# Two LayerNorms behind the residual adds, one row's residual moved to VectorE, one row's moments to ScalarE, in the token stage of a spectral and attention stack

## The chip, the cores and the metric

One core of one Trainium2 chip. The metric is the device time of the whole program in microseconds (us). The time before is 1554.5 us, the median of 3 runs from 1554.37 to 1554.54. The state of an execution (fast or slow) was judged by its time and granted clock.

## The reference

A stack of two kinds of layer, each with a LayerNorm and a residual, run twice: layer A is a two-dimensional Fourier transform, a product with complex weights and the inverse transform; layer B is attention over 64 segments that hand a memory of 8 rows on to each other.

```python
def _layernorm(x, axis=-1, eps=1e-05):
    m = jnp.mean(x, axis=axis, keepdims=True)
    v = jnp.var(x, axis=axis, keepdims=True)
    return (x - m) / jnp.sqrt(v + eps)

def _A_ref(x, w_r, w_i):                       # x: 1 x 2048 x 640
    X = jnp.fft.rfft2(x.astype(jnp.float32), axes=(-2, -1)) * (w_r + 1j * w_i)
    return jnp.fft.irfft2(X, s=(S, D), axes=(-2, -1)).astype(jnp.bfloat16)

# ... _B_ref: 64 segments of 32 rows, 32 heads of 128, memory of 8 rows ...
x = A_x
x = x + _A_ref(_layernorm(x), A_w_r, A_w_i)
x = x + _B_ref(_layernorm(x), B_mem0, ...)
x = x + _A_ref(_layernorm(x), A_w_r, A_w_i)
x = x + _B_ref(_layernorm(x), B_mem0, ...)
```

## The kernel before

The change touches the token stage, which is the end of layer A and the beginning of layer B. The 2048 tokens are 16 "rows" of 128 tokens by 640 columns. For each row TensorE does the last transform (`psg`, then `psy`, tiles in PSUM, the memory in which TensorE leaves its sums), the residual is added, mean and variance are taken, and the row is normalised and transposed for the projections of layer B. A "norm" here always means the two normalising passes of a pair of rows (norm 2 is rows 4 and 5), "inverse 2" the inverse root that norm 2 needs, and an evacuation is the copy of a finished transpose out of its PSUM buffer. The residual of a row can be added by TensorE (two matmuls with the identity, then a copy by ScalarE) or by VectorE, for the rows in `ADDED`. The moments of a row can be taken by VectorE (`bn_stats`, `bn_aggr`) or, for the rows in `SQUARED`, by a sum that the add gives as a by-product, scaled by GpSimd, and a Square on ScalarE.

```python
LEAD, LAG, EARLY, LAST = 0, 7, 10, 10
ADDED, SQUARED = (0, 1, 2, 3, 4, 6), (1, 3, 6) + (15,)

def tokens(s0):
    ...
    psy = pp.tile([128, 2, 512], FP32, name="psy", tag="pg", bufs=3)
    by_dve = s0 in ADDED
    for a in range(0 if by_dve else 2):
        nc.tensor.matmul(psy[:, a, 0:320], lhsT=g["ident"][:], rhs=x[:, s0, a * 320:(a + 1) * 320], start=True, stop=False)
    ...                                        # four transform matmuls into psy
    acc = nm[:, s0:s0 + 1] if s0 in SQUARED else None
    if by_dve and acc is None:
        nc.vector.tensor_tensor(out=xr, in0=psy[:, :, 0:320], in1=xr, op=ALU.add)
        flush()                                # bn_aggr of the row whose statistics are pending
    elif by_dve:
        nc.vector.scalar_tensor_tensor(out=xr, in0=psy[:, :, 0:320], scalar=1.0, in1=xr, op0=ALU.mult, op1=ALU.add, accum_out=acc)
        flush()
    elif acc is None:
        nc.scalar.copy(out=xr, in_=psy[:, :, 0:320])
    ...

def act_stats(s0):
    m, n = mv[s0 // 2][:, s0 % 2, :], nm[:, s0:s0 + 1]
    if s0 < 15:
        nc.gpsimd.tensor_scalar_mul(out=n, in0=n, scalar1=-D ** -1.5)
    ...
    nc.scalar.activation(out=xna[:, s0, :], in_=x[:, s0, :], func=ACTF.Square, scale=D ** -0.5, bias=n, accum_out=m[:, 1:2])
    nc.gpsimd.tensor_scalar_mul(out=m[:, 0:1], in0=n, scalar1=-D ** 0.5)

# _inverse, as GpSimd runs it for a pair of rows: six instructions on 128x2 elements
small.tensor_scalar_add(out=t, in0=v, scalar1=LN_EPS)
small.tensor_tensor(out=r0, in0=t, in1=g["half"][:, 0:t.shape[1]], op=ALU.pow)
...                                            # two products, one a*t+b, one product

with tc.manual_schedule(engines={nc.tensor.engine, nc.scalar.engine, nc.vector.engine}):
    moved, late, by_dve_jobs = [], [], False
    turn = lambda s0: s0 + (2 if LEAD <= s0 < LAG else 1)
    for i in range(16 + 1):
        held = moved if by_dve_jobs else []    # evacuations of the transposes of the step before
        for f in moved if not held else moved[:1]:
            f()
        held, moved = held[1:], []
        ...
        if not early and i % 2 == 1:
            norm((i - 5) // 2)                 # steps 11, 13, 15: norms 3, 4, 5
        if not last:
            ready(False)                       # statistics on VectorE
        if i < 16:
            spectrum_d(i)                      # psg of row i, and its copy by ScalarE
        ready(True)                            # moments on ScalarE
        for f in held:
            f()
            flush()
        for s0 in range(16):
            if turn(s0) == i:
                tokens(s0)
        if early and i >= 5 and i % 2 == 1:
            norm((i - 5) // 2)                 # steps 5, 7, 9: norms 0, 1, 2
        ...
        if i >= 4 and i % 2 == 0:
            inverse((i - 4) // 2, nc.gpsimd)
        ...
        if i >= 8 and i % 4 < 3:               # transposes of a group of four rows
            n = i % 4
            ...
```

The order of TensorE, ScalarE and VectorE is the order in which this is written; GpSimd's instructions are placed by a scheduler.

## Time and profile before

| | before |
|---|---|
| median of 3 runs | 1554.5 us |
| span of the profiled execution | 1552.9 us |
| granted TensorE clock | 0.999 |
| TensorE busy, whole span | 99% |
| the two token stages | 73 to 110 us and 835 to 872 us |

In a profile line of an engine's order of time, the first number is the start, the second the duration, then engine, source line, operation, output and inputs, shapes, count. A bracket at the end is idle time of the engine just before, with the instruction that ended it. In the chain of waits each line is one piece of the chain that ended last. PE is TensorE, DVE VectorE, ACT ScalarE, POOL GpSimd. L134 is the normalising pass, L633 the add with a sum, L630 the add without, L650 the statistics, L658 their aggregate, L663 GpSimd's scaling of a sum, L124 to L129 the inverse root on GpSimd, L607 the `psg` matmuls. Helpers that stand below the change have numbers one higher in the kernel after: L1676, L1680 and L1661 before are L1677, L1681 and L1662 after.

I use one yardstick from within a trace, the **stage length**: from the start of the first `psg` matmul to the start of the last normalising pass. Before, it is 33.16 us in the first token stage and 33.14 in the second.

### The profile page before, as it was taken

Reading aid. Unit: us, or ns where it says so; the run is one execution under the profiler, and the core shown is the slowest. Engines: PE = TensorE matmul, PEld = TensorE weight load, DVE = VectorE, ACT = ScalarE, POOL = GpSimd, SP = SyncE. Lnnn points to the kernel's source line nnn. Section 1 sums busy time; section 2 is a strip of 40 time slices with the busy share of each in tenths; the row PEclk is TensorE's granted clock in tenths of the full one; section 3 lists DMA queues with packets and bytes.
Section 4 is the critical chain, followed back from the end, with each engine's and each line's share of the span. In section 5 each row is a group of like instructions: output and inputs, shape, how many; then the busy total and the mean of one; then the engine's idle time right before and its main releaser. Section 6 shows DMA issues by size and latency. Waiting matters only on the chain.

```text
span 1552.9 us, 36725 instructions
## 1 busy us (share of the span) xinstructions
PE 1535.5 (99%) x14554; PEld 1081.3 (70%) x14555; DVE 816.6 (53%) x2418; ACT 764.9 (49%) x2229; POOL 246.0 (16%) x337
## 2 busy tenths in 40 slices
PE   9999999999999999999999999999999999999997
PEld 7776666666666666777777776666666666667775
DVE  7873555555556545632368545654556545553111
ACT  5574655556555565511126655556555565562000
POOL 2530111112111121100035201112111121110000
PEclk9999999999999999999999999999999999999999
DMA  4780343344533444645114523443434434337241
GB/s 173 230 299 27 111 170 122 137 140 135 178 123 136 136 136 149 201 117 162 51 54 159 178 83 125 136 150 121 172 124 140 148 125 166 124 107 228 79 127 53
DMA packets 168839, 214.90 MB, mean 138 GB/s; under 512 B 8144, under 2 KB 134360, under 8 KB 168656
## 3 DMA queue, kind: packets, MB, share of 16 engines
q1 hardware_dynamic: 168080, 210.15, 40.9%
q8 instruction: 116, 1.90, 0.5%
q0 software_dynamic: 576, 2.30, 0.4%
q14 instruction: 67, 0.55, 0.1%
HBM read 167.32 MB, written 45.10 MB: 137 GB/s over the span
## 4 chain that ended last, share of the span: by engine, by line
PE 92%; DVE 4%; POOL 1%; ACT 1%; issue 1%; DMA 0%; ACTq 0%; DVEq 0%; POOLq 0%
PE psv L1267 19%; PE psk L1201 19%; PE psx L1547 18%; PE psq L1201 18%; PE pso L1351 4%; PE pss L1277 4%; PE ab L449 2%; PE psl L1304 1%; PE psq L1225 1%; PE X L480 1%; PE psu L541 1%; DVE lnst L650 1%; PE psm L977 1%; PE psg L1708 1%; PE psvb L1640 1%
## 5 line engine op out<-in xcount | busy, mean ns | idle before, releaser
L1201 PEld LDWEIGHTS <-bB_S 128*128 128x128 bf16 x3180 | 261.5, 97 | 181.3 <-issue 1.1
L1260 DVE CAST bB_S<-psk 128x495 bf16<-128x495 f32 (+3 forms) x320 | 191.6, 599 | 281.3 <-PE psk L1201 276.9
L1547 PE MATMUL psx<-Wo_sb,bB_S 128*128 128x320 bf16 x2048 | 288.7, 299 | 0.1
L1280 ACT ACTIVATE bB_S<-pss 128x269 bf16<-128x269 f32 (+5 forms) x576 | 208.7, 387 | 138.3 <-PE pss L1277 137.9
L1547 PEld LDWEIGHTS <-bB_S 128*128 128x128 bf16 x2048 | 196.8, 98 | 73.9 <-DVE bB_S L1365 0.7
L1320 POOL TENSOR_TENSOR bB_S<-bB_S,bB_S 128x535 f32<-128x535 f32 x90 | 111.7, 1254 | 795.2 <-DVE bB_S L1312 762.2
L1245 ACT ACTIVATE bB_S<-psq 128x96 bf16<-128x96 f32 x300 | 152.1, 507 | 172.6 <-PE psq L1201 172.6
L1365 DVE TENSOR_TENSOR bB_S<-pso,bB_S 128x480 bf16<-128x480 f32 (+1 forms) x320 | 193.0, 603 | 55.8 <-PE pso L1351 47.2
L1281 DVE TENSOR_TENSOR bB_S<-bB_S,maskf 128x269 bf16<-128x269 bf16 (+5 forms) x576 | 159.5, 290 | 114.3 <-ACT bB_S L1280 114.3
L1269 ACT CAST bB_S<-psv 128x512 bf16<-128x512 f32 (+1 forms) x288 | 162.4, 564 | 81.0 <-PE psv L1267 81.0
L1267 PE MATMUL psv<-bB_S,B1hT_S 128*128 128x256 bf16 x1360 | 168.8, 272 | 0.0
L1267 PE MATMUL psv<-bB_S,B2hT_S 128*128 128x256 bf16 x1360 | 168.8, 272 | 0.0
L1201 PE MATMUL psk<-B1hT_S,bB_S 128*128 128x495 bf16 (+3 forms) x800 | 164.2, 343 | 0.0
L1201 PE MATMUL psk<-B2hT_S,bB_S 128*128 128x495 bf16 (+3 forms) x800 | 164.2, 343 | 0.0
L1201 PE MATMUL psq<-B1hT_S,bB_S 128*128 128x495 bf16 (+5 forms) x780 | 156.0, 336 | 0.5 <-DVE bB_S L1646 0.5
L1201 PE MATMUL psq<-B2hT_S,bB_S 128*128 128x495 bf16 (+5 forms) x780 | 156.0, 336 | 0.5 <-DVE bB_S L1646 0.5
L1267 PEld LDWEIGHTS <-B1hT_S 128*128 128x128 bf16 x1360 | 129.8, 98 | 24.3
L1267 PEld LDWEIGHTS <-B2hT_S 128*128 128x128 bf16 x1360 | 129.8, 98 | 24.3
L1277 PE MATMUL pss<-bB_S 128*128 128x132 bf16 (+8 forms) x1152 | 137.5, 219 | 0.0
L1277 PEld LDWEIGHTS <-bB_S 128*128 128x128 bf16 x1152 | 95.4, 97 | 55.1
L1351 PE MATMUL pso<-bB_S,bB_S 128*128 128x132 bf16 (+8 forms) x1152 | 118.6, 219 | 0.2
L1351 PEld LDWEIGHTS <-bB_S 128*128 128x128 bf16 x1152 | 89.7, 98 | 32.3 <-DVE oTmf L1366 1.9
(299 smaller groups left out, 1438.5 us busy)
## 6 DMA issues: line engine op xcount, KB each, us to landing
bB_S<-Rd SPq DMA_DIRECT2D x124, 535.0 KB
oTx_d<-bB_S SPq DMA_DIRECT2D x60, 512.0 KB
bB_S<-oTx_d SPq DMA_DIRECT2D x46, 512.0 KB
bB_S<-in_B_Wq_dram SPq DMA_DIRECT2D x32, 320.0 KB
bB_S<-in_B_Wk_dram SPq DMA_DIRECT2D x32, 320.0 KB
bB_S<-in_B_Wv_dram SPq DMA_DIRECT2D x32, 320.0 KB
Wo_sb<-in_B_Wo_dram SPq DMA_DIRECT2D x4, 1280.0 KB
B1wv_S<-in_B_Wv_dram SPq DMA_DIRECT2D x10, 512.0 KB
```

Source lines behind the costliest of these rows:

```text
L1201: nc.tensor.matmul(ps, lhsT=w[:, ch, hh * 128:(hh + 1) * 128], rhs=src[:, ch, lo:hi], start=(ch == 0), stop=(ch == 4))
L1245: nc.scalar.mul(out=qv[:, :, 0:SEG], in_=x_view(ps, o, n)[:, :, 1:SW], mul=scale)
L1260: nc.vector.tensor_copy(out=KTs[h % 2][:, lo:hi], in_=ps[:, 0:hi - lo])
L1267: nc.tensor.matmul(ps[:, i * 256:(i + 1) * 256], lhsT=hT[:, ch, st.hcol((t + i) * 128):st.hcol((t + i) * 128) + 128], rhs=w["Wv"][:, ch, : ...
L1269: nc.scalar.copy(out=V[:, t:t + n, :].rearrange("p a b -> p (a b)"), in_=ps[:, 0:n * 256])
L1277: nc.tensor.matmul(ps[:, off - o0:off - o0 + hi - lo], lhsT=KT[:, t * 128:(t + 1) * 128], rhs=QT[:, lo:hi], start=True, stop=True)
L1280: nc.scalar.activation(out=E[:, 0:n], in_=ps[:, 0:n], func=ACTF.Exp)
L1281: nc.vector.tensor_tensor(out=P[:, o0:o0 + n], in0=E[:, 0:n], in1=bs.mask[:, o0:o0 + n], op=ALU.mult)
L1320: nc.gpsimd.tensor_tensor(out=acc, in0=acc, in1=part, op=ALU.add)
L1351: nc.tensor.matmul(pso[:, lo - q0:hi - q0], lhsT=V[:, t, (h % 2) * 128:(h % 2 + 1) * 128], rhs=P[:, off:off + hi - lo], start=(i == 0), st ...
L1365: nc.vector.tensor_tensor(out=oT.rearrange("p (r s j) -> p r s j", r=16, j=2)[:, :, s0:s0 + ns, :], in0=byclass(po), in1=rx, op=ALU.mult)
L1547: self.tc.nc.tensor.matmul(ps[:, 0:320], lhsT=lhs(h, k // 2), rhs=self.g["Wo_sb"][:, h, c0:c0 + 320], start=(h == 0), stop=(h == H - 1))
```

## The change

The intent: TensorE, VectorE and GpSimd wait for each other in the middle of the stage, because a norm that waits for GpSimd stands in VectorE's queue ahead of the residual add that TensorE needs. So norms 0 and 1 go behind the adds of rows 4 and 6 (steps 6 and 8 rather than 5 and 7), the transposes of the first four rows one step later (9, 10, 11), row 5's residual goes from TensorE to VectorE, and row 4's moments from VectorE to ScalarE.

```diff
--- before.py
+++ after.py
@@ -608,7 +608,7 @@
             nc.scalar.copy(out=Gs[s0 % 3], in_=psg[:, :, 0:NF])
 
         LEAD, LAG, EARLY, LAST = 0, 7, 10, 10
-        ADDED, SQUARED = (0, 1, 2, 3, 4, 6), (1, 3, 6) + (15,)
+        ADDED, SQUARED = tuple(range(7)), (1, 3, 4, 6) + (15,)
         nm = wk.tile([128, 16], FP32, name="lnnm", tag="lnnm")
 
         def tokens(s0):
@@ -688,13 +688,14 @@
                 if late:
                     late.pop(0)()
                 last = i >= LAST
+                due = {6: 0, 8: 1}.get(i, (i - 5) // 2 if i >= 9 and i % 2 else None)
                 early = i < EARLY
                 done = [s0 for s0 in range(16) if turn(s0) == i - 1]
                 ready = lambda act: [stats(s0) for s0 in done if (s0 in SQUARED) == act and s0 < 15]
                 if last:
                     ready(False)
-                if not early and i % 2 == 1:
-                    norm((i - 5) // 2)
+                if not early and due is not None:
+                    norm(due)
                 if not last:
                     ready(False)
                 if i < 16:
@@ -706,8 +707,8 @@
                 for s0 in range(16):
                     if turn(s0) == i:
                         tokens(s0)
-                if early and i >= 5 and i % 2 == 1:
-                    norm((i - 5) // 2)
+                if early and due is not None:
+                    norm(due)
                 for f in late:
                     f()
                 late = []
@@ -722,8 +723,8 @@
                 if i == 16:
                     for s0 in range(10):
                         handoff.add_u(pp, xna[:, s0, :], s0)
-                if i >= 8 and i % 4 < 3:
-                    n = i % 4
+                if 9 <= i < 12 or i >= 12 and i % 4 < 3:
+                    n = i % 4 - (i < 12)
                     by_dve_jobs = n != 1 and i < 16
                     jobs = handoff.rows_out(handoff.rows_in(pp, xna, i // 4 - 2, 2 * n), by_dve_jobs)
                     if n == 1:
```

## The prediction

> **What bounds the kernel now.** I read the page first, then the chain of waits, then the order of time of each engine between 72 and 114 us.
>
> ```profile
> span 1552.9 us, 36725 instructions
> PE 1535.5 (99%) x14554; PEld 1081.3 (70%) x14555; DVE 816.6 (53%) x2418; ACT 764.9 (49%) x2229; POOL 246.0 (16%) x337
> PE 92%; DVE 4%; POOL 1%; ACT 1%; issue 1%; DMA 0%; ACTq 0%; DVEq 0%; POOLq 0%
> ```
>
> TensorE carries 92% of the chain, nearly all in attention, which the diff does not touch. The change is in the token stage, which runs twice. It begins with the first transform matmuls (psg) at 73.06 and 835.02 us and ends with the last row transposes near 110 and 872. What the two stages hold comes from the busy time by stretches:
>
> ```profile
> 73.00:110.00 37.00, 35.70 (x400) 26.03 (x398) 29.48 (x84) 29.01 (x56) 15.07 (x58) 1.00 0.87 299
> 835.00:872.00 37.00, 35.72 (x402) 26.05 (x400) 29.48 (x84) 29.02 (x56) 15.06 (x58) 1.00 0.86 300
> ```
>
> (Columns: length, then busy us with count of PE, PEld, DVE, ACT, POOL, then clock, DMA share, GB/s.) The stages are copies of each other: 74 us, 4.8% of the span. A 2% change of the whole, 31 us, would need 42% of them. So only "same" is in play, and the question is tenths of a microsecond.
>
> Within a stage the chain of waits passes TensorE, GpSimd (the norm's inverse root), then VectorE almost without a gap:
>
> ```profile
> 86.04 0.20 POOL lnrs L129
> 86.24 0.03 issue
> 86.27 0.45 DVE A1tok_S L134
> ...
> 91.29 0.20 POOL lnrs L129
> 91.49 0.03 issue
> 91.52 0.80 DVE A1tok_S L134 x2
> ...
> 101.38 0.76 DVE lnst L650 x2
> 102.13 0.34 DVE A1tok_S L134
> 102.48 0.13 DVE lnmv L658
> ```
>
> The reader should see that VectorE is the chain from 91.52 to 102.61 us. TensorE is near it, not ahead. Two idle times on VectorE lie before that, seen in its order of time:
>
> ```profile
> 82.58 0.80 DVE L134 TENSOR_SCALAR A1tok_S<-A1x_S,lnmv,lnrs 128x640 bf16<-128x640 bf16 x2 [0.69 <-POOL lnrs L129]
> 83.29 0.17 DVE L1626 COPY B1hT_S<-psm 128x40 bf16<-128x40 bf16 x1
> 83.38 0.17 DVE L1627 COPY gqf<-psm 128x5 bf16<-128x5 bf16 x1
> 83.45 0.82 DVE L630 TENSOR_TENSOR A1x_S<-psy,A1x_S 128x640 bf16<-128x640 f32 x1
> ...
> 86.27 0.45 DVE L134 TENSOR_SCALAR A1tok_S<-A1x_S,lnmv,lnrs 128x640 bf16<-128x640 bf16 x1 [1.08 <-POOL lnrs L129]
> ```
>
> Row 4's residual add stands behind the first norm, which waits for GpSimd until 82.54. The add frees a PSUM buffer that TensorE wants:
>
> ```profile
> 84.32 0.99 PE L607 MATMUL psg<-A1gt_S,A1UT_S 128*128 128x321 bf16 x6 [0.35 <-DVE A1x_S L630]
> ```
>
> That gap, 83.82 to 84.32 between issues, is the clearest one to win.
>
> **What the Trainium skill says.** (1) "TensorE: Matmul & The Clock Gate", its opening table of specifications: the queues of ScalarE, VectorE and GpSimd are strict first-in-first-out. The trace agrees: the add at 83.45 was runnable at about 82.3 and ran after the waiting norm. (2) "VectorE: DVE Perf Modes", section Why PSUM operands drop a tier: fp32 from PSUM runs at the basic rate. The trace agrees: the add takes 0.82 us for 640 columns, against 0.36 between issues for the norm's bf16 pass. (3) Same page, section Two Vector instructions with no wait between them: an accumulator output is a second instruction. The trace has it, 84 ns. (4) "SBUF — State Buffer", section SBUF: two separate sides: VectorE and GpSimd share one port pair as an exclusive lock. The trace agrees as far as it goes: GpSimd's tiny scaling of the sums took 0.43 us beside the norm pass at 82.6, and 0.23 elsewhere.
>
> **The change, part by part, for each stage.** I built the changed kernel and listed each engine's instruction order.
> - Row 5's residual moves from TensorE to VectorE. This takes away two identity matmuls at 0.137 us spacing (0.27) and one ScalarE copy (about 0.6 between issues), and gives VectorE an add of 0.82.
> - Row 4's moments move from VectorE to ScalarE: VectorE loses two statistics passes and an aggregate (0.80 + 0.12), gains an accumulator read (0.08); ScalarE gains a Square with read (0.82 between issues); GpSimd gains two small instructions (0.23 + 0.07 each).
> - Sums: TensorE -0.27, VectorE -0.02, ScalarE +0.2, GpSimd +0.6. So work hardly falls; what counts is the order.
> - Order: norm 0 now comes behind row 4's add (step 6), norm 1 behind row 6's add (step 8), both before the odd-step norm 2 at step 9. The first group's three transposes come one step later, in steps 9, 10, 11.
>
> Now I walk the new order by hand with the old durations. Up to 81.8 us nothing changes.
> - VectorE: row 4's last matmul issues at 82.03 and takes 0.30, so the add runs 82.36 to 83.2 rather than from 83.45. Then norm 0 (0.71) to 83.9, row 5's add to 84.75, row 5's statistics to 85.55, row 6's add to 86.4, aggregate to 86.5.
> - TensorE: row 5 without its residual ends issue at 83.54. The buffer was freed at 83.2, so the next psg starts at 83.54 in place of 84.32: 0.78 gained, of which 0.27 is removed work and 0.5 removed wait.
> - GpSimd: inverse 1 still needs row 3's Square (84.02), now with one row-4 instruction inside it: end 86.54, not 86.24. Norm 1 runs 86.57 to 87.3, hard behind row 6's add: the old 1.08 us wait is filled.
> - GpSimd then runs inverse 2 at once. It needs row 5's aggregate (86.5) and follows row 6's scaling: start about 86.93, plus the old length of this sequence with one instruction inside it (89.06 to 91.49, 2.43), end 89.37. So norm 2 starts about 89.40 instead of 91.52: 2.12 earlier. VectorE idles here, after row 7's statistics (88.07), for 1.3 us.
> - From norm 2 on, VectorE is full. Between norm 2's start and the first copy of the transposes of rows 4 to 7 the old kernel takes 91.52 to 96.63, 5.11. The new one has to do, additionally, the evacuation of the first transposes (two copies of 0.64, one of 0.25) and row 7's aggregate (0.12), and saves about 0.1 three times, where an aggregate or small copy no longer follows directly on what it reads: 5.11 + 1.65 - 0.3 = 6.46. It reaches the same point at 95.86, against 96.63: **0.8 us gained**.
> - From there both orders are the same to the end of the stage.
>
> TensorE must keep up. It reaches step 11's third transpose about 91.86, but that needs the buffer of the first, emptied by VectorE only at 92.6: a new stall near 0.8 us. After it TensorE finishes the transposes of rows 4 to 7 at about 94.97, against 95.84: 0.87 gained, just enough not to starve VectorE. ScalarE's last chain (row 15: copy, Square, logarithm, exponential) follows TensorE, 0.85 earlier. GpSimd's inverse 6 follows VectorE, 0.8 earlier. All three meet at the last two norms, so the whole tail moves by 0.8.
>
> Two stages, 2 x 0.8 = 1.6 us. Layer B begins when these end; the chain there shows no DMA, so the gain should pass through: 1554.5 - 1.6 = **1552.9 us**.
>
> **The rivals.**
> - The new wait eats it: TensorE stalls at step 11 for the transpose buffer. For: VectorE empties it behind norm 2. Against: VectorE is the later one anyway. If it is longer than I think by 0.5 us, VectorE starves and the gain falls to 0.3 a stage: 1553.9.
> - GpSimd becomes the bound: inverse 1 and 2 run back to back with four more small instructions in the two stages, and port collisions with norm passes doubled such instructions (0.43). For: norm 2 waits for it. Against: 2.1 us of lead. Three collisions of 0.2 would leave 0.2 a stage: 1554.1.
> - VectorE fuller than reckoned is no bound, and the 1.3 us idle before norm 2 closes better: if statistics and evacuation fall into it, the gain rises to about 1.3: 1551.9. Against: the queue is in order, and the evacuations are behind norm 2 in the listing.
> - Weight transfers set the end: DMA is 0.87 busy over the stage. Then nothing is gained: 1554.5. Against: the last prefetch pieces issue earlier, too, and the first projections after the stage waited for VectorE, not for a DMA.
>
> **Range and chances.** The steps are the same in both stages, so an error counts twice. I give my walk +-0.5 us a stage: 1551.9 to 1554.0, and widen to 1551.8 to 1554.3 for chip and collisions. The repeats of the old kernel spread only 0.17. Beyond 2% either way is practically excluded by the size of the stage: 0.5% each.
>
> **What would show it right or wrong.** Right: no gap before the psg at about 83.54; VectorE's first norm behind row 4's add, no GpSimd wait there; norm 2 near 89.4 after an idle of 1.3 us; a PE wait for a VectorE copy near 91.9; the last norm at 105.4 instead of 106.22; all of layer B shifted by 0.8, then 1.6, with equal durations. Wrong: norm 2 later than 90.2 (GpSimd), VectorE idle between 90 and 102 (TensorE or ScalarE starve it), or a DMA wait at the first query projections.

## The result, and the profile after

Five runs of the kernel after gave 1552.36 to 1552.75 us, median **1552.66**; the kernel before on the same chip gave 1554.35 to 1554.54, median 1554.5. The ratio is 0.9988 with a 95% interval of 0.9974 to 1.0003. A ratio is the mean time of one kernel's fast runs over that of the other's fast runs of the same rounds, so not quite the ratio of the medians. By the 2% criterion that is "same". The 1.84 us difference is small against that interval, but it stands in the trace: the span went from 1552.9 to 1550.9. All outputs are right.

A repeat on another chip gave 1552.54 us (before: 1554.4), and the stage lengths are steady:

| kernel | stage 1 | stage 2 |
|---|---|---|
| before | 33.16 | 33.14 |
| before, repeat | 33.20 | 33.17 |
| after | 32.14 | 32.12 |
| after, repeat | 32.11 | 32.10 |

So each stage is 1.02 us shorter. Between the stages nothing changed: from the start of the last normalising pass to the next stage's first `psg` it is 728.80 us before and 728.79 after.

The page of the kernel after, its first lines:

```profile
span 1550.9 us, 36721 instructions
PE 1533.7 (99%) x14550; PEld 1080.7 (70%) x14551; DVE 815.5 (53%) x2416; ACT 766.4 (49%) x2231; POOL 246.4 (16%) x341
```

Four matmuls fewer (two in each stage), two instructions more on ScalarE, four more on GpSimd. TensorE's busy time fell by 1.8 us, more than the work taken away, which is four identity matmuls at 0.137 us spacing, 0.55; the ends of matmuls are modelled, and I read no more from that difference.

VectorE in order of time, in the kernel after, in its first stage:

```profile
82.44 0.83 DVE L633 SCALAR_TENSOR_TENSOR A1x_S<-psy,A1x_S 128x640 bf16<-128x640 f32 x1 [0.35 <-PE psy L626]
...
83.19 0.80 DVE L134 TENSOR_SCALAR A1tok_S<-A1x_S,lnmv,lnrs 128x640 bf16<-128x640 bf16 x2
...
86.46 0.80 DVE L134 TENSOR_SCALAR A1tok_S<-A1x_S,lnmv,lnrs 128x640 bf16<-128x640 bf16 x2
...
89.28 0.45 DVE L134 TENSOR_SCALAR A1tok_S<-A1x_S,lnmv,lnrs 128x640 bf16<-128x640 bf16 x1 [1.23 <-POOL lnrs L129]
```

Row 4's add (82.44) no longer stands behind norm 0; norm 0 (83.19) starts with no wait for GpSimd, and norm 1 (86.46) with next to none: inverse 1 ends at 86.43, and the accumulator read of row 6's add at 86.38. The waits of 0.69 and 1.08 us that norms 0 and 1 had before are gone. In their place norm 2 waits 1.23 us for GpSimd, but it starts 2.24 us earlier on the clock of the trace than the 91.52 of before, and 2.33 earlier counted from the stage's start, which is at 73.15 here and at 73.06 before.

TensorE, in the kernel after, at the two places that the prediction named:

```profile
83.63 1.00 PE L607 MATMUL psg<-A1gt_S,A1UT_S 128*128 128x321 bf16 x6
...
92.56 0.38 PE L1662 MATMUL pstr<-ident,A1tok_S 128*128 128x128 bf16 x4 [0.60 <-DVE B1hT_S L1681]
```

The gap before the `psg` of 84.32 is closed (no bracket). A new one stands before the third of the first transposes, whose buffer VectorE empties late.

The chain of waits of the kernel after, from norm 2 to the stage's end:

```profile
89.05 0.21 POOL lnrs L129
89.26 0.03 issue
89.28 0.45 DVE A1tok_S L134
...
101.19 0.35 DVE A1tok_S L134
101.54 0.13 DVE lnmv L658
...
105.29 0.46 DVE A1tok_S L134
```

The chain hands over from GpSimd to VectorE at 89.28 and stays on VectorE to 101.67, as before it did from 91.52 to 102.61: VectorE's full stretch became longer, 12.39 us in place of 11.09.

**One sum holds for all the kernels.** In every trace except the last two the stage splits into three terms: (a) from the stage's start to the start of the accumulator read of row 6's add on VectorE (the end of that add, nearly); (b) from there to the start of norm 2, which is GpSimd's scaling of row 6's sum and inverse 2; (c) from norm 2 to the last pass. The accumulator read, before and then after:

```profile
88.58 0.09 DVE L633 DVE_READ_ACCUMULATOR A1x_S<-psy,A1x_S 128x1 f32 x1
```

```profile
86.30 0.08 DVE L633 DVE_READ_ACCUMULATOR A1x_S<-psy,A1x_S 128x1 f32 x1
```

| | (a) | (b) | (c) | stage |
|---|---|---|---|---|
| before | 15.52 | 2.94 | 14.70 | 33.16 |
| after | 13.15 | 2.98 | 16.01 | 32.14 |

So (a) gained 2.37, (b) lost 0.04, and (c) lost 1.31: net 1.02. Row 6's add comes earlier, and over half of what that gives is paid back, because the evacuation of the first transposes, which was done while VectorE would have waited, now lies behind norm 2.

### The profile page after: what moved, and what is told of

Its sections match the earlier page's. It is cut to its first block, busy times and chain, and to the rows that moved or that the text cites. A ratio compares the mean times of both kernels' runs of the same rounds, so it can differ in the third digit from the quotient of the medians.

```text
span 1550.9 us, 36721 instructions
## 1 busy us (share of the span) xinstructions
PE 1533.7 (99%) x14550; PEld 1080.7 (70%) x14551; DVE 815.5 (53%) x2416; ACT 766.4 (49%) x2231; POOL 246.4 (16%) x341
## 4 chain that ended last, share of the span: by engine, by line
PE 93%; DVE 3%; ACT 1%; POOL 1%; issue 1%; DMA 0%; DVEq 0%; ACTq 0%; POOLq 0%
PE psv L1268 19%; PE psk L1202 19%; PE psx L1548 18%; PE psq L1202 18%; PE pso L1352 4%; PE pss L1278 4%; PE ab L449 2%; PE psl L1305 1%; PE psq L1226 1%; PE psg L607 1%; PE X L480 1%; PE psu L541 1%; PE psm L978 1%; PE psg L1709 1%; DVE lnst L650 1%
```

## The experiments

Theory at the outset: the order does it. Norms 0 and 1 behind the adds let row 6's add come 2.4 us earlier; the two rows that change engine are of little worth by themselves. Rivals: the moved rows matter (less work on TensorE, or VectorE relieved before row 6's add), or the deferral of norm 0 alone, which frees TensorE's buffer, is the gain.

The first four kernels ran on one chip, where the kernel before took 1553.89 us.

### The order alone

```diff
 # kernel after, but
-ADDED, SQUARED = tuple(range(7)), (1, 3, 4, 6) + (15,)
+ADDED, SQUARED = (0, 1, 2, 3, 4, 6), (1, 3, 6) + (15,)
```

> The new order alone (norm 0 in step 6, norm 1 in step 8, the first group's transposes one step later); which engine adds and measures rows 4 and 5 is as before. My theory: the gain is VectorE reaching its full stretch (norm 2) earlier, and that comes from the order alone: row 4's add before the norm that waits for GpSimd, norm 1 behind row 6's add. By hand: row 4's add 82.4, norm 0 to 84.0, statistics of row 4 and 5 to 85.6, row 6's add to 86.4, so norm 2 near 89.2 as in the changed kernel: 1552.7 us. Rival (the moved rows carry it, by 0.27 us of TensorE a stage and 0.6 of ScalarE): at most half of the gain is left, 1553.6 us or more.

Measured: 1553.35 us, ratio 0.9996 (0.9982 to 1.001); stage 32.66 and 32.65. The order alone gives 0.50 of the 1.02 us. My theory that it does all fell. Row 6's add ends 0.34 us later than in the kernel after, since row 5's statistics wait for ScalarE's copy of row 5 (VectorE runs row 4's aggregate alone in that time), and GpSimd's step (b) is 3.19 rather than 2.98. The cause of the second is in GpSimd's order of time; first the kernel with the order alone:

```profile
86.53 0.43 POOL L663 TENSOR_SCALAR lnnm<-lnnm 128x1 f32<-128x1 f32 x1 [0.69 <-DVE A1x_S L633]
```

and the kernel after, the same instruction:

```profile
86.51 0.22 POOL L663 TENSOR_SCALAR lnnm<-lnnm 128x1 f32<-128x1 f32 x1
```

It is the scaling of row 6's sum; it starts 0.05 us after norm 1's first pass in both (86.48 and 86.46) and takes twice as long in one of them.

### Row 5's residual on VectorE alone, old order

```diff
 # kernel before, but
-ADDED, SQUARED = (0, 1, 2, 3, 4, 6), (1, 3, 6) + (15,)
+ADDED, SQUARED = tuple(range(7)), (1, 3, 6) + (15,)
```

> Only row 5's residual on VectorE, all else as before. My theory: TensorE is not the bound of the stage, VectorE keeps its wait for the norm at 86.27, the extra add fits into the wait before it: 1554.5 us, +-0.2. Rival (TensorE's work counts): two identity matmuls less in each stage, 2 x 0.27: 1554.0 us or less.

Measured: 1554.4 us (1554.03 to 1555.3), ratio 1.0003; stage 33.08 and 32.88. By itself it gives 0.08 to 0.26 us a stage, all of it in (a): 15.45 and 15.24. (b) and (c) are 2.93 and 14.70, as before. The two stages differ by 0.2 us because of one instruction of GpSimd, the scaling of row 3's sum, first stage, then second:

```profile
82.81 0.43 POOL L663 TENSOR_SCALAR lnnm<-lnnm 128x1 f32<-128x1 f32 x1
```

```profile
844.67 0.23 POOL L663 TENSOR_SCALAR lnnm<-lnnm 128x1 f32<-128x1 f32 x1
```

Both start 0.05 us after norm 0's first pass (82.76 and 844.62). So row 5's add alone is worth about 0.08 us a stage, and the 0.26 of the second stage holds 0.2 from this scaling. The median is 0.5 us above the kernel before on this chip although both stages are shorter; the kernel before was not traced on this chip, the ratio's interval is 0.999 to 1.0017, and nothing is drawn from that difference.

### Row 4's moments on ScalarE alone, old order

```diff
 # kernel before, but
-ADDED, SQUARED = (0, 1, 2, 3, 4, 6), (1, 3, 6) + (15,)
+ADDED, SQUARED = (0, 1, 2, 3, 4, 6), (1, 3, 4, 6) + (15,)
```

> Only row 4's moments on ScalarE, all else as before. My theory: GpSimd gets one small instruction inside inverse 1 (0.3 us), norm 1 and row 6's add come 0.3 later, norm 2 too: slower by 0.3 a stage, 1555.1 us. Rival (0.9 us less on VectorE a stage is what counts): faster, 1553.5 us or less.

Measured: 1557.26 us (1555.66 to 1559.81), ratio 1.0023 (1.0009 to 1.0036); stage 34.01 and 35.64. It is a loss. ScalarE in order of time in this kernel, then TensorE:

```profile
86.17 0.83 ACT L666 ACTIVATE A1tok_S<-A1x_S,lnnm 128x640 bf16<-128x640 bf16 x1 [1.70 <-POOL lnnm L663]
...
87.00 0.67 ACT L636 CAST A1x_S<-psy 128x640 bf16<-128x640 f32 x1
```

```profile
87.72 0.43 PE L622 MATMUL psy<-A1x_S,ident 128*128 128x320 bf16 x2 [1.97 <-ACT A1x_S L636]
```

and GpSimd:

```profile
85.91 0.23 POOL L663 TENSOR_SCALAR lnnm<-lnnm 128x1 f32<-128x1 f32 x1
```

GpSimd's scaling of row 4's sum was scheduled into the middle of inverse 1 and ran only at 85.91, though the sum was there at 84.15. ScalarE's Square of row 4 waits 1.70 us for it, ScalarE's copy of row 5, queued behind, comes at 87.00, and TensorE waits 1.97 us for the buffer. That is the price of a queue in order with one late operand. The direction was expected, the size (0.3 us a stage) and the rest of the mechanism were not: norm 1 did come 0.30 later (13.51 us into the stage against 13.21), but row 6's add came 0.78 later, behind ScalarE. The second stage, longer by another 1.6 us, ran at a granted clock of 0.96 from 837 to 875 us of this trace; why, I can't say, and I draw nothing from it. The fastest of the five runs, 1555.66 us at a clock of 0.999, is 1.77 us above the kernel before, about twice the 0.85 of the first stage; the median holds more than the change.

### Norm 0 behind row 4's add alone

```diff
 # kernel before, but
+due = {6: 0}.get(i, (i - 5) // 2 if i >= 7 and i % 2 else None)
-if not early and i % 2 == 1:
-    norm((i - 5) // 2)
+if not early and due is not None:
+    norm(due)
 # ... and the same for the early norms; transposes and rows as before
```

> Only norm 0 one step later, behind row 4's add; norm 1 stays in step 7, transposes and rows as before. My theory on the extra 0.2 us a stage that my prediction lacked: GpSimd's scaling of row 3's sum (0.43 us at 82.63) ran against norm 0's pass on VectorE, which started 0.05 before it; with norm 0 later it takes 0.23, row 3's Square starts 0.2 earlier, and inverse 1, norm 1 and norm 2 are 0.2 earlier: 1554.1 us. Rival (the 0.43 has nothing to do with norm 0; chance of the queue): still 0.43 and 1554.5 us.

Measured: 1553.79 us, ratio 0.9999; stage 32.96 and 32.93, 0.20 less than before. That is right in size. GpSimd, in the kernel before, then in this one:

```profile
82.63 0.43 POOL L663 TENSOR_SCALAR lnnm<-lnnm 128x1 f32<-128x1 f32 x1
```

```profile
82.58 0.23 POOL L663 TENSOR_SCALAR lnnm<-lnnm 128x1 f32<-128x1 f32 x1
```

The scaling of row 3's sum takes 0.23 us when no norm pass runs beside it. Before, norm 0 did (82.58). Everything behind it, row 3's Square and inverse 1, comes that much earlier. But the freed TensorE buffer as such gives nothing here (the `psg` behind it starts at 83.77, 0.51 earlier in its stage than before): norm 1 still stands ahead of row 6's add and waits for inverse 1:

```profile
86.03 0.45 DVE L134 TENSOR_SCALAR A1tok_S<-A1x_S,lnmv,lnrs 128x640 bf16<-128x640 bf16 x1 [1.38 <-POOL lnrs L129]
```

The wait merely became 1.38 us, from 1.08. So norm 0's deferral is worth 0.2, and what the order gives beyond that needs norm 1 behind row 6's add.

### The kernel after again, and each moved row alone with the new order

These and the first of the two improved versions below ran on another chip, where the kernel before took 1554.4 us. The first is a plain repeat of the kernel after.

> The changed kernel once more, on this call's chip, because the kernel before differed by 0.6 us between two chips. I compare stages within one trace: from the first transform matmul (psg) to the start of the last norm pass, 33.16 and 33.14 us before, 32.14 and 32.12 after. Expected again: 32.13 +-0.1 in both stages, and 1.8 to 2.1 us under the kernel before of the same chip. Rival (part of the gain was the chip): under 1.2 us.

Measured: 1552.54 us, ratio 0.9989 (0.9975 to 1.0002); stage 32.11 and 32.10. As expected.

```diff
 # kernel after, but row 5's residual stays on TensorE
-ADDED, SQUARED = tuple(range(7)), (1, 3, 4, 6) + (15,)
+ADDED, SQUARED = (0, 1, 2, 3, 4, 6), (1, 3, 4, 6) + (15,)
```

> New order and row 4's moments on ScalarE, but row 5's residual left on TensorE and ScalarE. Theory (the gain is when row 6's add ends on VectorE): ScalarE now does Square of rows 3 and 4 before it copies row 5, so row 5's statistics start near 85.85, row 6's add ends a us later than in the changed kernel, norm 2 too: stage 33.0 to 33.3, the gain gone. Rival (each moved row brings its own share, 0.25 a stage): stage 32.4.

Measured: 1555.91 us, ratio 1.001 (0.9996 to 1.0024); stage 33.51 and 33.50. VectorE in order of time:

```profile
86.10 0.89 DVE L650 BATCH_NORM_STATS2 lnst<-A1x_S 128x6 f32<-128x320 bf16 x2 [1.93 <-ACT A1x_S L636]
```

ScalarE now squares rows 3 and 4, one after the other, before its copy of row 5; VectorE's statistics of row 5 wait 1.93 us for that copy, and row 6's add stands behind them.

```diff
 # kernel after, but row 4's moments stay on VectorE
-ADDED, SQUARED = tuple(range(7)), (1, 3, 4, 6) + (15,)
+ADDED, SQUARED = tuple(range(7)), (1, 3, 6) + (15,)
```

> New order and row 5's residual on VectorE, but row 4's statistics left there, too. Theory: VectorE has 0.8 us more before row 6's add, and the gain shrinks by 0.6 to 0.9 a stage: stage 32.75 to 33.0. Rival (each moved row brings its own share): stage 32.4.

Measured: 1554.97 us, ratio 1.0003; stage 33.13 in both. VectorE has row 4's statistics more to do ahead of row 6's add: (a) is 13.93 rather than 13.15, and (b) is 3.19, with the long scaling again.

The stage lengths as a table of the parts (first stage):

| | neither row | row 5's add only | row 4's Square only | both |
|---|---|---|---|---|
| old order | 33.16 | 33.08 | 34.01 | not run |
| new order | 32.66 | 33.13 | 33.51 | 32.14 |

The two rows are a pair: with the new order each alone loses 0.47 or 0.85 us, together they gain 0.52. The reason lies in what stands before row 6's add. A residual of row 5 on VectorE costs an add of 0.82 there, row 4's moments on ScalarE take 0.92 away, and row 5's copy must leave ScalarE for the Square of row 4 to have room there.

### Is GpSimd's inverse 2 the path? A dose on it

These ran on a third chip with the kernel before at 1554.23 us.

```diff
 # kernel after, in inverse(q, small), behind _ln_inverse
+if q == 2:
+    for _ in range(2):
+        small.tensor_scalar_mul(out=rs[q][:, 0:2], in0=rs[q][:, 0:2], scalar1=1.0)
```

> A dose on GpSimd: the changed kernel with two more small multiplications by 1.0 at the end of inverse 2, each about 0.19 us and 0.08 between. Theory (norm 2 waits for GpSimd's inverse 2, and VectorE sets the end from norm 2 on): norm 2 starts 0.55 later, and the stage goes from 32.12 to 32.65 us or so, all of the dose. Rival (TensorE is the bound from step 11 on): stage at most 32.3.

Measured: 1553.36 us, ratio 0.9994; stage 32.76 and 32.74. VectorE:

```profile
89.65 0.45 DVE L134 TENSOR_SCALAR A1tok_S<-A1x_S,lnmv,lnrs 128x640 bf16<-128x640 bf16 x1 [1.85 <-POOL lnrs L674]
```

The two instructions put norm 2 back by 0.63 us, and the stage became 0.62 longer. VectorE's wait grew from 1.23 to 1.85. All of it passes to the end, so norm 2's wait for GpSimd is on the path in the kernel after, and nothing downstream has slack for it.

### Is TensorE's saved work of worth? A dose on it

```diff
 # kernel after: TensorE does row 5's identity matmuls again; the transform then overwrites them, so the result stays right
-for a in range(0 if by_dve else 2):
-    nc.tensor.matmul(psy[:, a, 0:320], lhsT=g["ident"][:], rhs=..., start=True, stop=False)
+for a in range(0 if by_dve and s0 != 5 else 2):
+    nc.tensor.matmul(psy[:, a, 0:320], lhsT=g["ident"][:], rhs=..., start=True, stop=by_dve)
```

> A dose on TensorE: the changed kernel with the two identity matmuls of row 5 put back, their result thrown away (the next matmul starts the sum anew); ScalarE's and VectorE's work as in the changed kernel, result right. Theory (the 0.27 us of matmuls saved is no part of the gain): TensorE is 0.27 later until its wait of 0.60 at the third transposes, which shrinks to 0.3; stage 32.12 +-0.05. Rival (TensorE's saving is part of the gain): stage 32.4.

Measured: 1553.02 us, ratio 0.9991; stage 32.53 and 32.52. The expectation that nothing would change fell; the rival is right. 0.27 us of TensorE's time costs 0.40. (a) is 0.20 longer, since VectorE and TensorE are nearly level at row 5's add in the kernel after (row 5's last matmul ends at 83.79 there, and the add starts at 83.91). GpSimd is level there, too: in the kernel after inverse 1 ends at 86.43 and row 6's add at 86.38, and the scaling of row 6's sum, which comes behind both, starts at 86.51. And (b) is 0.21 longer, since GpSimd's scaling of row 6's sum falls beside norm 1 in the long form. GpSimd in this kernel:

```profile
86.33 0.42 POOL L663 TENSOR_SCALAR lnnm<-lnnm 128x1 f32<-128x1 f32 x1 [0.26 <-DVE A1x_S L633]
```

### A plain repeat of the kernel before, as a trace from another chip

> The kernel before, for its trace on another chip: the yardstick of the stage should not depend on the chip: 33.15 +-0.05 in both stages, whatever the whole time is.

Measured: 1554.48 us in one run (state unknown), stage 33.20 and 33.17. The stage length repeats within 0.04 us on another chip, as expected.

### A better version: norm 2 a step later

VectorE's wait of 1.23 us before norm 2 is idle time on the path, and the statistics of row 8 and an evacuation stand behind it, ready. So norm 2 goes to step 10.

```diff
 # kernel after, but
-due = {6: 0, 8: 1}.get(i, (i - 5) // 2 if i >= 9 and i % 2 else None)
+due = {6: 0, 8: 1, 10: 2}.get(i, (i - 5) // 2 if i >= 11 and i % 2 else None)
```

> Meant as an improvement: the changed kernel with norm 2 in step 10, behind the first copy of the transposes and row 8's statistics, which fill the 1.23 us for which VectorE waited for GpSimd. By hand: copy 88.2 to 88.8, row 8's statistics 89.15 to 89.9, norm 2 with no wait, third transposes of TensorE without their 0.6 us wait for a buffer; VectorE 0.85 us earlier at the transposes of rows 4 to 7. Stage 31.3 us, 1.7 us less in all than the changed kernel. Rival (TensorE or ScalarE becomes the bound, or norm 3 comes too late for the transposes): stage 31.8 to 32.1.

Measured: 1551.51 us (1550.8 to 1551.95), ratio 0.9981 (0.9967 to 0.9995); stage 31.40 in both. That is 2.89 us under the kernel before and 1.03 under the kernel after on the same chip (1.7 was expected, and twice the stage's gain would be 1.4); by the 2% criterion it is "same", too. VectorE in order of time:

```profile
88.30 0.74 DVE L1677 COPY B1hT_S<-pstr 128x480 bf16<-128x480 bf16 x1 [0.18 <-PE pstr L1662]
...
90.02 0.43 DVE L134 TENSOR_SCALAR A1tok_S<-A1x_S,lnmv,lnrs 128x640 bf16<-128x640 bf16 x1
```

An evacuation and row 8's statistics fill the old wait, and norm 2 at 90.02 has no bracket. TensorE's wait at the third transposes has gone, too:

```profile
91.88 0.38 PE L1662 MATMUL pstr<-ident,A1tok_S 128*128 128x128 bf16 x4
```

### A last refinement: all of the evacuations of that step first

In the version above VectorE still waits 0.29 us ahead of row 8's statistics (between the end of the aggregate's issue at 88.93 and 89.22).

```diff
 # version above, but
-held = moved if by_dve_jobs else []
+held = moved if by_dve_jobs and i != 10 else []
```

> This is the version before it (norm 2 a step later, at the end of step 10) with all of the first group's evacuations of step 10 moved ahead of row 8's statistics on VectorE, into the 0.29 us that VectorE still waited for there. If that wait was free time on the chain, the stage shortens from 31.40 to about 31.1 us, some 0.3 us twice, and the whole time by about 0.5 us. Rival: GpSimd's inverse 3, which needs row 7's aggregate, comes later by the same evacuations, so norm 3 waits for it and the stage stays at 31.4 us or becomes longer.

Measured: 1551.1 us (1550.75 to 1551.29; before 1554.32), ratio 0.9979 (0.9965 to 0.9993); stage 31.38 and 31.35 as against 31.40. The wait of 0.29 is filled, but the stage stays the same: the rival was right. Row 7's aggregate now comes behind both evacuations, so GpSimd starts inverse 3 late:

```profile
90.06 0.23 POOL L124 TENSOR_SCALAR lnrs<-lnmv 128x2 f32<-128x2 f32 x1 [0.92 <-DVE lnmv L658]
...
92.11 0.20 POOL L129 TENSOR_TENSOR lnrs<-lnrs,lnnb 128x2 f32<-128x2 f32 x1
```

Inverse 3 ends at 92.31 and norm 3 starts at 92.34, right behind it, 19.28 us into the stage; in the version above it started 19.31 us into it, with inverse 3 long done. The 0.4 us between the two medians is within what chips and rounds differ by, as the stages show.

## Why the prediction was right

The predicted time, 1552.9 us, stands against 1552.66 measured, within the range. Point by point:

- **The bound and the size.** Right. The change only moves the token stage, "same" was the only outcome in play, layer B kept its durations, and the two stages' gains add up: 2 x 1.02 = 2.04 us in the spans' 2.0.
- **Row 4's add, norm 0 and the `psg` behind them.** Right to 0.01 us. The add was predicted at 82.36 and starts at 82.44 in a trace whose stage starts 0.09 later; `psg` was predicted at 83.54 and starts at 83.63.
- **Norm 1 hard behind row 6's add.** Right within 0.1 us: that add was to end at 86.4, and its accumulator read starts at 86.30 and takes 0.08, in a trace whose stage starts 0.09 later.
- **Norm 2.** Predicted 2.12 us earlier, measured 2.33. The term that was mis-sized is GpSimd's inverse 1, which I took over from the old trace with row 3's scaling at 0.43 us. I had named that figure as a collision with norm 0 and then forgot that the change takes norm 0 away from there. The deferral of norm 0 alone shows it: 0.23 us and a stage 0.20 shorter. Another 0.2 came right by luck, as far as is known: the walk gave row 6's scaling, right behind the start of norm 1, its short length, and only the second rival named the chance of the long one. It is short in the kernel after (0.22), but not with the order alone, with either row alone or with the dose on TensorE (0.42 to 0.43).
- **The repayment behind norm 2.** Predicted 1.35 (6.46 against 5.11), measured 1.31.
- **The new wait of TensorE at the third transposes.** Predicted from 91.86 with 0.8 us, measured from 91.96 to 92.56, 0.60: TensorE arrived as predicted, and VectorE freed the buffer sooner, with norm 2. It did not starve VectorE. The dose on GpSimd made it 1.23 us, and even then the stage grew by no more than norm 2 was put back.
- **"What counts is the order".** Only half right, and the prediction's number did not depend on it. The order alone is worth 0.50 us of 1.02; the two rows carry the other half, and only as a pair. My sums of work (TensorE -0.27, VectorE -0.02) were not checked by the page's busy times, in which records overlap, and they said little: what matters is which engine is relieved *ahead of row 6's add*, and by how much. I had also held TensorE's saving for unimportant, because the walk made VectorE the later one. Putting it back cost 0.40.
- **The rivals.** Transfers did not set the end. GpSimd is on the path before norm 2, as the walk had it, but without the three collisions of the second rival (one is there, 0.34 us for row 4's scaling at 83.36 beside norm 0, and GpSimd idles 0.28 us behind it). The third rival, work falling into the wait before norm 2, did not come about in this kernel: the evacuation and row 8's statistics stand behind norm 2 in VectorE's order and ran behind it. Written into the order, it is the better version, and it is worth more than that rival said: 1.76 us a stage from the kernel before, not 1.3 (2.89 in the whole time, not 2.6).

The improved version's 31.40 us is thus the same argument carried one norm further.

**Left open.** The combination of both rows with the old order was not run. The later transposes of the first four rows were never run apart from the later norms. Why GpSimd's scaling beside norm 1 takes 0.22 us in the kernel after and its repeat, but 0.43 with the order alone, with either row alone and with the dose on TensorE, is not settled: it starts 0.05 us after the first pass in the first kernel and in the second. It is worth 0.2 us a stage. For row 6's scaling behind norm 1 the short form came each time that GpSimd went to it straight from inverse 1, the long one each time that GpSimd had stood idle; but row 3's scaling in the kernel with row 5's add alone came straight from inverse 0 in both stages and took 0.43 in one and 0.23 in the other. The duration of the pair of passes does not tell who gave way: it is 0.80 with the scaling of 0.43 in the kernel before (82.58), and 0.80 with 0.22 in the kernel after (86.46).

## What to carry to other kernels

In an in-order queue, put work that waits for a slow helper behind the work that others wait for, then look at what the next such wait would let in: moving norms 0 and 1 gave 0.5 us a stage (1.0 with the two rows), moving norm 2 as well another 0.7. Judge a change of engine by what it takes away ahead of the one instruction that the chain runs through, not by sums over the stage: two moves that each lost 0.5 to 0.9 us gained 0.5 together. And when an old duration is carried into a new order, ask whether the neighbour that stretched it is still there.

## What the Trainium skill lacked or had wrong

- "SBUF — State Buffer", section Who interferes with whom, says that VectorE in a two-port mode and GpSimd exclude each other for a whole instruction, by order of issue. The runs agree in part: the scaling of 0.23 us takes 0.43 beside a norm pass (before at 82.63, with the order alone at 86.53, with the dose on TensorE at 86.33). But in the kernel after it takes 0.22 at the same 0.05 us behind the pass, and the kernel with row 5's add alone has 0.43 in its first stage (82.81) and 0.23 in its second (844.67). The page gives no way to tell which of two instructions that start so close together wins, and the starts in the records do not tell it.
- "GPSIMD Engine Reference", section Elementwise — side-by-side cycle accounting, gives per-element costs and measured cases of 512 and 2048 elements, but none for tiny operands, where this kernel has its path: on 128x1 or 128x2 elements, with no norm pass beside them, a product takes 0.20 us, an add or a scaling 0.19 to 0.23, and a power 0.72, with about 0.08 us between dependent ones. No page has the power.
- "ScalarE: Activation LUTs" mentions an accumulator output, but not that it is a second instruction in the trace: 0.18 to 0.19 us in its record, 0.09 until the next instruction starts.
